# Differences of inputs, some low parts of weights and the last group's sums on VectorE, and other times for the weight and input tasks

## The chip, the cores and the metric

The kernel runs on one core of a Trainium2 chip. The metric is the device time of one execution in microseconds (us), lower is better. The kernel before took 955.99 us in the median of three runs (955.51 to 956.83). One more execution was taken with the profiler; all views below are of that one.

## What is computed

Three parts follow each other: attention with exponential features over 4 batches, 8 heads, 576 positions and 64 dimensions, then two two-layer networks on the 2304 tokens of width 512 that come out of it, with an inner width of 2048. All of it is float32.

```python
def phi(x):
    proj = np.einsum('bhsd,df->bhsf', x, w_phi)
    proj = proj - np.max(np.abs(proj), axis=-1, keepdims=True)
    return np.concatenate([np.exp(proj), np.exp(-proj)], axis=-1)
...
num = np.einsum('bhsf,bhfd->bhsd', phi(q), np.einsum('bhsf,bhsd->bhfd', phi(k), v))
x = num / (den + 1e-6)          # then tokens x 512
h = x @ w_in;   x = (h * sigmoid(h)) @ w_out      # first network
h = x @ w2_in;  y = (h * cos(h)) @ w2_out         # second network
```

## The kernel before, in words

**The three parts.** Attention fills the first 167 us or so and is not touched by the change, but tasks of the first network already run between its pieces. The two networks are the two layers of `moe` (layer 0 and layer 1 in the code; the text calls them layer 1 and layer 2). Nearly all of the span after attention is matmuls of TensorE (PE).

**Precision and products.** A float32 operand is held as two reduced-precision tiles: a high part, which is a copy into the type `fp32r`, and a low part, which is the operand minus the high part. A product then takes three matmuls (high-high, high-low, low-high; `products`, lines 746 to 753). The first matrix product of a layer is done with a Strassen-like scheme of seven block products instead of eight. The scheme needs sums and differences of blocks on both sides: of the weights (`S1`, `S2`, `S3`, `S4`, made by `add` inside `in_tasks`, line 230, in the tile `stage`) and of the tokens (`T1` to `T4`, made by `diff` inside `Inputs.build`, line 560, in tiles `tt`). Each of them is then split into a high part, which the scalar engine (ACT) copies, and a low part: for weights in `Weights.split` (ACT line 186, low part line 189 on GpSimd, POOL), for tokens in `split` inside `Inputs.build` (ACT line 570, low part line 573 on VectorE, DVE, in tiles `xo`).

**The order of the steps.** The inner width is cut in four groups (`NG` = 4). For each layer the token blocks 0, 1 and a small one run through the four groups, then the blocks 2 and 3. One block in one group is a step (`step`, line 910; `small`, line 885, for the small block). A step makes its seven products in PSUM tiles `h`, applies the activation (`act`; in layer 2 the cosine goes over DVE line 776, ACT line 777, and DVE lines 780 to 782), and multiplies by the second weight matrix into tiles `y`, which are added into `xa` (ACT line 854 for the first group, DVE line 856 after that). Inside a step ACT copies the first product into a second bank as soon as it is there (line 936); the third product that PE starts waits for that copy. DVE sums two banks in lines 954 and 965.

**What sets the order on the engines.** The kernel's schedule is written by hand (`manual_schedule`): each engine executes in the order in which the program issues. Beside the steps there are tasks: converting weights from the 64-bit inputs (`convert`: ACT line 166, DVE lines 167, 172 and 178), summing and splitting them (tasks named "in" for the first matrix and "out" for the second, with `put` making the two parts and saving them to DRAM), and building token blocks ("build0", "build1", "buildS"). A clock `weights.now` counts 7 units in a step and 4 in a small step, `at[layer, group, block]` is its value at a step's start. At certain points of a step `fill()` runs all tasks whose time has come, in order of time; a task can also ask that another was done a number of units ago (`after`). If a weight or a token block is needed and not made yet, its tasks are run on the spot. So the times that `plan` (line 998) gives to the tasks decide where in the queues of ACT, DVE, POOL and SyncE (SP) their instructions stand.

```python
def fill():
    weights.flush()
    loads()
    tasks.run(weights.now)
    weights.now += 1
```

The layer-2 weights (`STORED`) are converted while the last group of layer 1 runs, the last quarter of them in layer 2, and are read back from DRAM.

## Time and profile before

| | |
|---|---|
| three runs, median | 955.99 us (955.51 to 956.83) |
| profiled execution | 956.93 us |
| its span on the core | 955.1 us |
| mean granted TensorE clock | 0.996 of full speed |
| chain that ended last, by engine | PE 85%, DVE 7%, ACT 2%, DMA 2%, POOL 1% |

The span is what the profiler sees between the first and the last instruction; the device time is 1.8 us longer. Busy time is the sum of an engine's instruction durations; PEld is the load of weights into TensorE, which overlaps with the matmuls. The chain is followed back from the last instruction, at each step to what released it; a share of a chain is not a saving. A wait in the list of waits is idle time of an engine just before an instruction, put down to the event that came last. Rows of a timeline show in brackets how long the engine was idle before, and who released it.

### The profile page before, as it was taken

The page shows a single profiled execution, that of the slowest core. Times are in us where ns is not written, and L with a number is a line of the kernel's source. Part 1 is how long each engine was busy: PE and PEld are TensorE (multiplying, and loading weights), DVE is VectorE, ACT ScalarE, POOL GpSimd, SP SyncE. Part 2 cuts the span into 40 slices and gives each one's busy share as a digit, 9 for nine tenths or more (in the row PEclk, how much of TensorE's full clock was granted, in tenths as well). Part 3 has the DMA queues.
Part 4 walks back from the last instruction along what each step waited for, and adds up shares of the span by engine and source line. Part 5 has one row for each costly group of instructions (what it writes and reads, how often), then busy time and mean ns, then how long its engine had stood idle before and what let it go on. Part 6 is the DMA issues. An engine that isn't in the chain of part 4 may idle for free.

```text
span 955.1 us, 18114 instructions
## 1 busy us (share of the span) xinstructions
PE 935.0 (98%) x7271; PEld 817.4 (86%) x7271; DVE 635.1 (66%) x913; ACT 520.4 (54%) x944; POOL 237.8 (25%) x190
## 2 busy tenths in 40 slices
PE   8999999899999999999999999999899999999998
PEld 7777776788899898889988898988789898888996
DVE  5777566785737558965465667488876778566556
ACT  4667766665535355565544456564554556644442
POOL 0112352335433423822502621002320120000000
PEclk9999999999999999999999999999999999999999
DMA  5653655566636479797797866352538366242302
GB/s 166 207 142 102 192 171 143 189 224 233 219 151 237 162 228 337 272 324 293 292 323 267 303 252 239 132 178 89 192 133 271 121 232 216 99 171 89 132 1 88
DMA packets 95492, 186.53 MB, mean 195 GB/s; under 512 B 27953, under 2 KB 56753, under 8 KB 94641
## 3 DMA queue, kind: packets, MB, share of 16 engines
q1 hardware_dynamic: 95264, 185.25, 57.0%
q8 instruction: 57, 0.93, 0.4%
q14 instruction: 27, 0.21, 0.1%
q10 hardware_dynamic: 144, 0.13, 0.0%
HBM read 128.06 MB, written 57.22 MB: 194 GB/s over the span
## 4 chain that ended last, share of the span: by engine, by line
PE 85%; DVE 7%; DMA 2%; ACT 2%; issue 2%; POOL 1%; SPq 0%; DVEq 0%; POOLq 0%; ACTq 0%
PE h L752 34%; PE y L828 6%; PE y L827 6%; PE y L826 6%; PE y L821 6%; PE y L823 6%; PE y L822 6%; PE p L377 3%; PE num L455 3%; PE kv L436 3%; PE t L407 2%; PE num L466 2%; DVE xo L573 2%; PE kv L433 1%; PE t L369 1%
## 5 line engine op out<-in xcount | busy, mean ns | idle before, releaser
L752 PEld LDWEIGHTS h<-xo,w 128*128 128x128 f32 x2688 | 332.1, 189 | 20.1 <-ACT h L936 7.1
L752 PE MATMUL h<-xo,w 128*128 128x256 f32 x2688 | 337.7, 282 | 9.7 <-ACT h L936 5.7
L821 PE MATMUL y<-gh,w 128*128 128x512 f32 (+1 forms) x320 | 119.5, 374 | 1.9 <-ACT xa L854 1.4
L823 PE MATMUL y<-gh,w 128*128 128x512 f32 (+1 forms) x320 | 118.8, 371 | 0.0
L822 PE MATMUL y<-gl,w 128*128 128x512 f32 (+1 forms) x320 | 118.7, 371 | 0.0
L828 PE MATMUL y<-w,gl 128*128 128x512 f32 x288 | 113.9, 396 | 0.0
L827 PE MATMUL y<-w,gh 128*128 128x512 f32 x288 | 113.6, 394 | 0.0
L826 PE MATMUL y<-w,gh 128*128 128x512 f32 x288 | 113.4, 394 | 0.0
L189 POOL TENSOR_TENSOR w<-wt,w 128x512 fp32r<-128x512 f32 x32 | 45.9, 1437 | 235.7 <-ACT w L186 220.7
L777 ACT ACTIVATE tb<-tb 128x512 f32<-128x512 f32 x72 | 45.6, 634 | 99.1 <-DVE tb L776 99.1
L772 DVE TENSOR_TENSOR gl<-ta,gh 128x512 fp32r<-128x512 f32 x72 | 63.9, 888 | 53.5 <-ACT gh L770 53.4
L189 POOL TENSOR_TENSOR w<-stage,w 128x512 fp32r<-128x512 f32 x56 | 78.1, 1402 | 74.9 <-ACT w L186 57.2
L776 DVE SCALAR_TENSOR_TENSOR tb<-tb,ta 128x512 f32<-128x512 f32 x72 | 52.2, 725 | 55.8 <-ACT tb L786 55.8
L856 DVE TENSOR_TENSOR xa<-y,xa 128x512 f32<-128x512 f32 (+1 forms) x114 | 70.1, 656 | 26.3 <-PE y L823 19.7
L821 PEld LDWEIGHTS y<-gh,w 128*128 128x128 f32 x320 | 60.2, 188 | 11.8 <-ACT xa L854 1.6
L823 PEld LDWEIGHTS y<-gh,w 128*128 128x128 f32 x320 | 60.1, 188 | 11.4 <-POOL w L189 0.2
L822 PEld LDWEIGHTS y<-gl,w 128*128 128x128 f32 x320 | 60.1, 188 | 9.3
L828 PEld LDWEIGHTS y<-w,gl 128*128 128x128 f32 x288 | 54.0, 188 | 13.2 <-DVE gl L782 0.4
L827 PEld LDWEIGHTS y<-w,gh 128*128 128x128 f32 x288 | 54.0, 188 | 10.7
L826 PEld LDWEIGHTS y<-w,gh 128*128 128x128 f32 x288 | 54.1, 188 | 10.5
L770 ACT CAST gh<-ta 128x512 fp32r<-128x512 f32 x72 | 44.7, 621 | 24.9 <-PE y L823 23.0
L782 DVE TENSOR_TENSOR gl<-tb,gh 128x512 fp32r<-128x512 f32 x72 | 52.8, 733 | 2.8
(102 smaller groups left out, 1411.0 us busy)
## 6 DMA issues: line engine op xcount, KB each, us to landing
w<-d SPq DMA_DIRECT2D x48, 512.0 KB, 5.6
raw_in<-in_moe_w_in SPq DMA_DIRECT2D x32, 512.0 KB, 5.0
raw_out<-in_moe_w_out SPq DMA_DIRECT2D x32, 512.0 KB, 4.9
d<-w SPq DMA_DIRECT2D x32, 512.0 KB, 4.7
rb<-rd SPq DMA_DIRECT2D x16, 288.0 KB, 4.2
va<-in_v SPq DMA_DIRECT2D x32, 128.0 KB, 6.0
yd<-xa SPq DMA_DIRECT2D x4, 1024.0 KB, 4.4
xo<-yd SPq DMA_DIRECT2D x32, 128.0 KB, 6.1
```

The lines of the kernel that those rows point to most:

```text
L189: nc.gpsimd.tensor_sub(lo, t, hi.bitcast(F32))
L752: nc.tensor.matmul(dst[:, ab], w[:, a, ab, c * P:(c + 1) * P], o[:, b, idx, c], start=start and n == 1, stop=n == 12, skip_group_check=True)
L772: return [silu, lambda: nc.vector.tensor_sub(lo, a, hi.bitcast(F32))]
L776: nc.vector.scalar_tensor_tensor(b, b, MAGIC, a, op0=ALU.subtract, op1=ALU.subtract)
L782: nc.vector.tensor_sub(lo, b, hi.bitcast(F32))
L821: nc.tensor.matmul(o, w[:, 0, at], hi[:, f, x], stop=False, **st)
L822: nc.tensor.matmul(o, w[:, 0, at], lo[:, f, x], start=False, stop=False)
L823: nc.tensor.matmul(o, w[:, 1, at], hi[:, f, x], start=False, stop=en)
L826: nc.tensor.matmul(o, hi[:, f, at], w[:, 0], stop=False, **st)
L827: nc.tensor.matmul(o, hi[:, f, at], w[:, 1], start=False, stop=False)
L828: nc.tensor.matmul(o, lo[:, f, at], w[:, 0], start=False, stop=en)
L856: nc.vector.tensor_tensor(v, o, v, op=ALU.add)
```

## The change

The change touches the engine and the time of work beside the products. All four differences of a token block now go to DVE (line 563; before, DVE did two of them for blocks 0 and 1 of layer 1, POOL the rest). The low parts of weights (line 189) go to DVE while the clock is between 0 and the first small step, which are the first two steps, and from one unit after the start of layer 2; elsewhere they stay on POOL. The sums of weights (line 232) go to DVE in the second of these times only. The rest of the change gives other start and end times to the tasks, and the first difference of a token block that is loaded from DRAM asks for 3.5 units after its load instead of 4; since the clock only counts whole units between the calls, this acts as 4.

```diff
@@ class Weights
+        self.lows, self.sums_at = (), ()
...
@@ split
-        nc.gpsimd.tensor_sub(lo, t, hi.bitcast(F32))
+        e = nc.vector if any(a <= self.now < b for a, b in self.lows) else nc.gpsimd
+        e.tensor_sub(lo, t, hi.bitcast(F32))
...
@@ in_tasks, add
-                (nc.gpsimd.tensor_sub if minus else nc.gpsimd.tensor_add)(at(o), at(a), at(b))
+                e = nc.vector if any(a <= self.now < b for a, b in self.sums_at) else nc.gpsimd
+                (e.tensor_sub if minus else e.tensor_add)(at(o), at(a), at(b))
...
@@ Inputs.build
-        def diff(n, a, b, engine):
+        def diff(n, a, b):
             def go():
                 tmp[n] = temps()
-                engine.tensor_sub(part(n), part(a), part(b))
+                nc.vector.tensor_sub(part(n), part(a), part(b))
...
-        d, g = nc.vector if dram is None else nc.gpsimd, nc.gpsimd
-        t1, t2, t4, t3 = diff("T1", "12", "11", d), diff("T2", "22", "T1", d), diff("T4", "21", "T2", g), diff("T3", "22", "12", g)
+        t1, t2, t4, t3 = diff("T1", "12", "11"), diff("T2", "22", "T1"), diff("T4", "21", "T2"), diff("T3", "22", "12")
         if loads:
-            after(loads[-1], 4, t1)
+            after(loads[-1], 3.5, t1)
...
@@ moe
+        weights.lows = (0, at[0, 0, SMALL]), (at[1, 0, 0] + 1, n)
+        weights.sums_at = weights.lows[1:]
...
@@ plan
-                    a, b = at[0, NG - 1, 0] + 2, at[0, NG - 1, 3] + 2
-                    ends = (a + (b - a) * g / 3, a + (b - a) * (g + 1) / 3) if g < 3 else (at[1, 0, SMALL], at[1, 2, SMALL])
+                    a, b = at[0, NG - 1, 0] + 2.5, at[0, NG - 1, 3] + 3
+                    ends = (a + (b - a) * g / 3, a + (b - a) * (g + 1) / 3) if g < 3 else (at[1, 0, SMALL] - 4, at[1, 2, SMALL] - 1)
...
-                tasks.add("in", ins[:12], *((b0 + 1, b1 - 1) if (l, g) != (0, 1) else (b0 + 6, b1 + 3)))
-                tasks.add("in", ins[12:21], b1 - 1, b1 + 6)
-                tasks.add("in", ins[21:], b1 + 6, bs + 3)
-                tasks.add("out", outs[:3], b1, b1 + 6)
-                tasks.add("out", outs[3:], bs + 1, nx + 6.5)
+                tasks.add("in", ins[:12], *((b0 + 2.5, b1 + 5) if (l, g) != (0, 1) else (b0 + 6.5, b1 + 6.5)))
+                tasks.add("in", ins[12:21], b1 - 3, b1 + 6)
+                tasks.add("in", ins[21:], b1 + 8.5, bs + 1)
+                tasks.add("out", outs[:3], b1 - 2, b1 + 7.5)
+                tasks.add("out", outs[3:], bs + 0.5, nx + 6.5)
...
-            tasks.add("build1", b[2:], 3, 8)
+            tasks.add("build1", b[2:], -2.5, 7)
...
-            for tag, src, used, start in (((0, 2), xd[2], at[0, l, 0], at[0, l, 1] + 2),
-                                               ((0, 3), xd[3], at[0, l, 1], at[0, l, SMALL] + 2),
-                                               ((1, 0), yd[0], at[0, l, 2], at[0, l, 3] + 1),
-                                               ((1, 1), yd[1], at[0, l, 3], at[1, 0, 0]),
-                                               ((1, 2), yd[2], at[1, l, 0], at[1, l, 1] + 2),
-                                               ((1, 3), yd[3], at[1, l, 1], at[1, l, SMALL] + 2)):
+            for tag, src, used, start, end in (((0, 2), xd[2], at[0, l, 0], at[0, l, 1] + 2, 5.5),
+                                               ((0, 3), xd[3], at[0, l, 1], at[0, l, SMALL] + 2, 9.5),
+                                               ((1, 0), yd[0], at[0, l, 2], at[0, l, 3] + 3, 1),
+                                               ((1, 1), yd[1], at[0, l, 3], at[1, 0, 0] + 1, 8),
+                                               ((1, 2), yd[2], at[1, l, 0], at[1, l, 1] + 0.5, 4.5),
+                                               ((1, 3), yd[3], at[1, l, 1], at[1, l, SMALL] - 2, 10)):
...
-                tasks.add(name, b[4:], start, start + 7)
-            for n, t in enumerate((at[0, 0, 1] + 2, at[0, 0, 3])):
+                tasks.add(name, b[4:], start, start + end)
+            for n, t in enumerate((at[0, 0, 1] + 2.5, at[0, 0, 3] + 1.5)):
...
-        for name, n, end in (("in", 1, 0), ("out", 2, 6)):
+        for name, n, end in (("in", 1, 0), ("out", 2, 6.5)):
...
-            tasks.add(name, todo[n:], 3, end)
+            tasks.add(name, todo[n:], 2.5, end)
```

In the listings below a row is a line of the program, an operation, out<-in and the shape; lines of the changed kernel are 1 to 5 higher for the same statement (563 is 566, 573 is 576, 167 is 168, 172 is 173, 178 is 179, 189 is 191, 232 is 235, 305 and 308 are 308 and 311, 772 is 777, 776 is 781, 780 to 782 are 785 to 787, 854 is 859, 936 is 941, 965 is 970).

**First excerpt: DVE in the second step** (layer 1, group 0, block 1). `xo_2452` is this block's tile of high and low parts, `xn` and `rb` belong to the last head of attention, `wt` and `stage` to weights. Before:

```order
L573 TENSOR_TENSOR xo_2452<-xa,xo_2452 128x512
L178 SCALAR_TENSOR_TENSOR wt<-ws,wt 128x512
L772 TENSOR_TENSOR gl<-ta,gh 128x2x256
L573 TENSOR_TENSOR xo_2452<-tt,xo_2452 128x512
L167 TENSOR_SCALAR wt<-raw_out 128x512
L172 SCALAR_TENSOR_TENSOR wt<-raw_out,wt 128x512
L305 TENSOR_TENSOR xb<-xn,rb 128x4x128 x2
L308 TENSOR_TENSOR xa<-xn,rb 128x2x64
L573 TENSOR_TENSOR xo_2452<-xa,xo_2452 128x512
```

Of the change:

```order
L576 TENSOR_TENSOR xo_2452<-xa,xo_2452 128x512
L576 TENSOR_TENSOR xo_2452<-tt,xo_2452 128x512
L566 TENSOR_TENSOR tt<-xa 128x512
L191 TENSOR_TENSOR w_2449<-wt,w_2449 128x512
L168 TENSOR_SCALAR wt<-raw_out 128x512
L173 SCALAR_TENSOR_TENSOR wt<-raw_out,wt 128x512
L308 TENSOR_TENSOR xb<-xn,rb 128x4x128 x2
L311 TENSOR_TENSOR xa<-xn,rb 128x2x64
L576 TENSOR_TENSOR xo_2452<-xa,xo_2452 128x512
L179 SCALAR_TENSOR_TENSOR wt<-ws,wt 128x512
L576 TENSOR_TENSOR xo_2452<-tt,xo_2452 128x512
L168 TENSOR_SCALAR stage<-raw_in 128x2x256
```

The block's third low part (its second from `xa`) is the last row before and the first row of the change: it has moved ahead of the three operations of attention's last head. A difference and a low part of a weight (`w_2449`) are new on this queue, and the row after these is a further low part, `w_2450`.

**Second excerpt: ACT after the small block's step of the first group.** The rows of lines 854 and 859 bring the output products to `xa`; the `w_` rows are copies of weights. Before:

```order
L854 COPY xa<-y 128x4x128 x2
L186 CAST w_2651<-wt 128x512
L186 CAST w_2652<-stage 128x512
L186 CAST w_163<-stage 128x512
L186 CAST w_164<-stage 128x512
L186 CAST w_165<-stage 128x512
L166 ACTIVATE ws<-raw_out 128x512
L769 ACTIVATE ta<-h 128x512
L770 CAST gh<-ta 128x2x256
L854 COPY xa<-y 128x4x128 x2
```

Of the change:

```order
L859 COPY xa<-y 128x4x128 x2
L187 CAST w_2655<-stage 128x512
L187 CAST w_2656<-stage 128x512
L187 CAST w_2657<-wt 128x512
L167 ACTIVATE ws<-raw_out 128x512
L774 ACTIVATE ta<-h 128x512
L775 CAST gh<-ta 128x2x256
L859 COPY xa<-y 128x4x128 x2
L187 CAST w_2658<-stage 128x512
L187 CAST w_163<-stage 128x512
L187 CAST w_164<-stage 128x512
L187 CAST w_165<-stage 128x512
```

Three copies instead of five stand between the two evacuations, and four follow the second one.

**Third excerpt: DVE in layer 2**, in the part of the first group that holds the longest wait. `tb`, `gh` and `gl` are tiles of the cosine, `stage` holds the weights to be summed. Before:

```order
L776 SCALAR_TENSOR_TENSOR tb<-tb,ta 128x512
L780 TENSOR_TENSOR tb<-tb,u 128x512
L781 CAST gh<-tb 128x2x256
L782 TENSOR_TENSOR gl<-tb,gh 128x2x256
L167 TENSOR_SCALAR wt<-raw_out 128x512
L776 SCALAR_TENSOR_TENSOR tb<-tb,ta 128x512
```

Of the change:

```order
L781 SCALAR_TENSOR_TENSOR tb<-tb,ta 128x512
L168 TENSOR_SCALAR wt<-raw_out 128x512
L785 TENSOR_TENSOR tb<-tb,u 128x512
L786 CAST gh<-tb 128x2x256
L787 TENSOR_TENSOR gl<-tb,gh 128x2x256
L235 TENSOR_TENSOR stage<-stage 128x512
L781 SCALAR_TENSOR_TENSOR tb<-tb,ta 128x512
```

A sum of weights has come to the place ahead of the second cosine step, and the shift of line 167 stands earlier.

## Rows read from the trace of the kernel before

**Rows 1.** The page's part 1: engine, busy us (share of the span), instructions.

```profile
PE 935.0 (98%) x7271; PEld 817.4 (86%) x7271; DVE 635.1 (66%) x913; ACT 520.4 (54%) x944; POOL 237.8 (25%) x190
```

**Rows 2.** Busy time by stretches; columns in the first line.

```profile
core 0: us, PE busy (x) PEld busy (x) DVE busy (x) ACT busy (x) POOL busy (x), PEclk, DMA share, GB/s
165.00:200.00 35.00, 30.52 (x228) 26.19 (x217) 27.92 (x42) 24.19 (x45) 13.24 (x11) 1.00 0.64 202
200.00:230.00 30.00, 28.61 (x184) 25.88 (x183) 19.28 (x24) 18.25 (x33) 17.91 (x12) 1.00 0.61 224
230.00:370.00 140.00, 140.00 (x940) 128.59 (x939) 86.89 (x132) 71.90 (x127) 47.88 (x36) 1.00 0.60 211
370.00:415.00 45.00, 43.48 (x302) 39.98 (x301) 41.17 (x48) 26.81 (x49) 31.41 (x21) 1.00 0.88 303
415.00:560.00 145.00, 145.00 (x903) 130.09 (x902) 81.64 (x116) 71.71 (x126) 48.45 (x34) 1.00 0.83 298
560.00:585.00 25.00, 23.95 (x157) 21.61 (x157) 19.74 (x31) 15.96 (x27) 6.06 (x4) 1.00 0.73 274
672.00:700.00 28.00, 24.90 (x151) 22.53 (x151) 20.96 (x28) 15.52 (x26) 8.40 (x6) 0.94 0.41 154
700.00:800.00 100.00, 100.00 (x622) 89.20 (x621) 76.92 (x115) 50.86 (x82) 16.30 (x12) 1.00 0.59 195
```

**Rows 3.** PE's waits: line waited for: us in total, times, longest us.

```profile
PE h L752 <- ACT h L936: 5.7, 4, 3.1
PE h L752 <- DVE xo L573: 2.1, 2, 1.7
PE y L821 <- ACT xa L854: 1.4, 1, 1.4
```

**Rows 4.** Timeline of PE in the first step: start, duration, instruction, [idle before].

```profile
171.82 5.94 PE L752 MATMUL h<-xo,w 128*128 128x256 f32 x48 [0.68 <-ACT h L936]
178.55 0.62 PE L752 MATMUL h<-xo,w 128*128 128x256 f32 x3 [0.78 <-DVE u L965]
```

**Rows 5.** Busy time (columns as in rows 2) after two of PE's waits.

```profile
580.84:585.38 4.54, 4.54 (x37) 4.54 (x38) 3.15 (x6) 3.56 (x6) 0.00 (x0) 1.00 0.82 307
691.29:697.35 6.06, 6.06 (x37) 6.06 (x38) 2.60 (x5) 3.50 (x6) 1.28 (x1) 0.72 0.28 116
```

**Rows 6.** Instructions on tile tt: ns min/median/max, first and last start.

```profile
L573 DVE TENSOR_TENSOR xo<-tt,xo x32: 676/684/1787, 163.9 to 799.4; 128x512 fp32r<-128x512 f32 x32
L563 POOL TENSOR_TENSOR tt<-xo x12: 1292/1302/1677, 356.6 to 792.0; 128x512 f32<-128x512 f32 x12
L563 DVE TENSOR_TENSOR tt<-xa x2: 685/686/686, 156.0 to 172.2; 128x512 f32<-128x512 f32 x2
```

**Rows 7.** Timeline ahead of the longest wait, all engines (columns as in rows 4).

```profile
681.77 1.78 DVE L776 SCALAR_TENSOR_TENSOR tb<-tb,ta 128x512 f32<-128x512 f32 x1
...
684.80 1.29 POOL L189 TENSOR_TENSOR w<-stage,w 128x512 fp32r<-128x512 f32 x1 [1.80 <-ACT w L186]
...
684.98 1.41 DVE L781 CAST gh<-tb 128x512 fp32r<-128x512 f32 x1
...
686.06 3.14 POOL L232 TENSOR_TENSOR stage<-stage 128x512 f32<-128x512 f32 x2
...
686.42 1.67 DVE L782 TENSOR_TENSOR gl<-tb,gh 128x512 fp32r<-128x512 f32 x1
...
688.00 1.48 DVE L167 TENSOR_SCALAR wt<-raw_out 128x512 int32<-128x512 int32 x1
...
690.66 0.58 ACT L936 COPY h<-h 128x512 f32<-128x512 f32 x1
```

**Rows 8.** ACT's waits (columns as in rows 3).

```profile
ACT h L936 <- PE h L752: 65.2, 25, 5.0
...
ACT w L186 <- POOL stage L232: 11.3, 8, 2.4
...
ACT xo L570 <- POOL tt L563: 7.8, 5, 4.2
```

**Rows 9.** Timeline of ACT, the weight copies behind the small block's products.

```profile
219.33 0.62 ACT L186 CAST w<-stage 128x512 fp32r<-128x512 f32 x1 [2.00 <-POOL stage L232]
```

## The prediction

> **What bounds the kernel now.** The page's busy times come first: TensorE (PE) is busy 935.0 of 955.1 us [rows 1], so nothing that leaves its matmuls alone can save more than 20 us, and the question is where its idle 20 us lie. The table by stretches answers it for the two layers. PE is idle 35.00 - 30.52 = 4.48 us from 165 to 200, 1.39 us from 200 to 230, 1.52 us from 370 to 415, 1.05 us from 560 to 585 and 3.10 us from 672 to 700 [rows 2]; in the stretches between them that the same table shows, PE has no idle time up to 800. The list of PE's waits names who ended them: the ScalarE (ACT) copy of line 936 four times for 5.7 us, the VectorE (DVE) low part of line 573 twice for 2.1 us and an ACT evacuation (line 854) once for 1.4 us [rows 3]. No weight load is in that list.
>
> Two of these waits belong to the first step, where PE has nothing else to do between a product and its copy: 0.68 us at 171.82 for the copy of line 936 and 0.78 us at 178.55 for the DVE sum of line 965 [rows 4]. Their order does not change, so they stay. That leaves 4.48 - 0.68 - 0.78 = 3.02 us in the first stretch.
>
> The longest wait costs more than itself. From 691.29, when it ends, 37 matmuls take 6.06 us at a mean granted clock of 0.72; the same 37 after the 1.05 us wait at 580.84 take 4.54 us at full clock [rows 5]. So 6.06 - 4.54 = 1.52 us are the price of running at 1.2 GHz instead of 2.4 for a while after 3.10 us of idleness, and they go with the wait.
>
> **Why these engines are late.** One DVE operation of 128x512, the low part from a difference, takes 0.684 us in the median and 1.787 us at worst; a difference takes 0.685 us on DVE and at least 1.292 us on GpSimd (POOL) [rows 6]. The slow DVE cases are those beside POOL work. From 684.98 to 689.4 a cast, a subtraction and a shift take 1.41, 1.67 and 1.48 us, while POOL does a low part (684.80) and two sums of the last weight group (686.06, 3.14 us); only then does the DVE step of line 776 start, and the ACT copy that PE waits for starts at 690.66 [rows 7]. Two-input operations on POOL thus cost twice: their own time and about 1 us of each DVE operation that they meet. ACT also waits on POOL directly: 7.8 us for differences (longest 4.2) and 11.3 us for sums [rows 8].
>
> **The change, part by part.** It moves 48 operations from POOL to DVE: 28 differences (all of them), 16 low parts of weights (5 in the first two steps, 11 in layer 2) and the 4 sums of the last group. No matmul, copy or DMA is added or removed; PE's order is the same, while weight work, saves and weight loads shift by a few places in the queues of ACT, DVE, POOL and SyncE (SP).
>
> *First two steps, 165 to 200.* Without POOL work here the stretched operations fall back to 0.68, and the low part that PE awaited at 190.41 now stands ahead of three operations of the attention's last head (first excerpt). The third moved low part (w_2450) stands on DVE behind an ACT copy that is itself behind three ACT operations of some 0.62 us (as the weight copy in [rows 9]), so DVE is held up to 1.9 us, with the sum of line 965 behind it. This costs PE between 0 and 1.9 us; I take 0.5, the lower part, as PE has output products to do before it needs that sum. Gain 3.02 - 0.5 = 2.5 us.
>
> *Small block, 200 to 230.* The evacuation is late because ACT's queue holds five weight copies before it, and one of them waits 2.00 us for POOL's sum of line 232 [rows 9]. In the new order three stand there, and four more come after it (second excerpt). Gain 1.39 us. The weights they make are then some 3 us later, but PE needs them only in the middle of the next step. Bounds: nothing, or 1.39 us.
>
> *Differences of stored blocks.* In 370 to 415 six differences leave POOL's 21 operations and come to DVE, which is busy 41.17 of 45 us [rows 2]. They add 6 x 0.69 = 4.1 us and take off about as many stretches of 1 us, so DVE's load hardly moves; what goes is the round trip DVE, POOL, ACT, DVE. I take half of the 1.52 us: 0.76, between 0 and 1.52. In 560 to 585 POOL's differences are all of its work, DVE has 5 us free, and the 1.05 us wait (an ACT copy behind a cast that waited for a POOL difference) goes whole. A difference on DVE could also hold that queue for its block's load: each stands two evacuations into the following step, by which time POOL had long had the data, so this costs nothing here; if a load were late, everything of DVE behind it would be.
>
> Against this part speaks a rule. The row is DVE's 91% from 370 to 415. The Trainium skill, "Perfetto Trace Analysis", section "Optimizing Scalar/DVE Operations", says that work may be offloaded to GpSimd if DVE is saturated, and that it might not help between these two because they share a read port. By its first half this part would cost 4.1 us instead of giving 0.76; by its second half it would give about 0. The trace bears out the second half in the stretched operations.
>
> *Layer 2, 560 to 800.* Low parts and sums of the last group go to DVE, so POOL has nothing left after about 560. A sum costs DVE 0.69 where it met about 1 us of stretching per sum before. The chain from 681.77 has eight steps (line 776, ACT's sine, lines 780, 781 and 782, one sum, line 776, sine; third excerpt). At an unstretched 0.69 us each [rows 6] it ends at 687.3, the copy of 0.58 us [rows 7] at 687.9, and PE wants it at 691.29 - 3.10 = 688.2. The wait of 3.10 and the 1.52 of half clock go: 4.62 us. The bound below is nothing, if another wait takes its place. The 11 low parts add 11 x 0.69 = 7.6 us to a DVE that has far more idle time there, 23 us between 700 and 800 alone [rows 2]; I cost them at nothing, and their waits on ACT are the slower rival.
>
> *Task times* move sums later (1.5 units after the small block begins) and builds closer together; I cost these at nothing beyond the above.
>
> Sum: 2.5 + 1.39 + 0.76 + 1.05 + 4.62 = 10.3 us. The profiled execution took 956.93 us, so 946.6. It lies 0.94 above the median of the runs shown; I keep this as an allowance for one new wait of the common size (0.85 to 1.05 us) and forecast **946.6 us**.
>
> **Rivals.**
> *The long wait stays* (chance 0.14). The copy of line 936 still stands behind an ACT sine that waits for DVE's line 776, and a sum now stands just before that (third excerpt). For it: DVE is in order and each low part waits for ACT. Against it: the unstretched chain has 0.3 us to spare, and more if its cast is shorter than 0.69. Then 10.3 - 4.62 = 5.7 us remain: 951.2 us.
>
> *DVE becomes the bound from 370 to 415* (0.11). The 4.1 us come on top, with no stretch given back, because POOL keeps its 15 weight operations there. Gain 10.3 - 0.76 - 4.1 = 5.4: 951.5 us. The first half of the sentence from the Trainium skill's "Perfetto Trace Analysis" would have it so.
>
> *Nothing lasting* (0.05). POOL keeps 72 of 88 low parts, and the moved times make as many waits as they end: about 956.
>
> *Slower: low parts hold DVE* (0.07). A low part on DVE waits for its ACT copy, which can stand behind the copy of line 936, and ACT waits there for PE 65.2 us in 25 waits, 2.6 us each [rows 8]. In layer 2 the DVE operations behind are those that ACT's sine and PE's next products need. If all 11 passed on the full 2.6 us, that would be 28.7 us; from 0.94 us each it outweighs the gain. With half of it, 14.3 us, the time is 956.9 - 10.3 + 14.3 = 961. Against it: in the order read, such a low part is followed by a step of line 776 that waits for a later ACT operation anyway.
>
> **The numbers.** The forecast has 0.63. A measurement of this kernel can tell about 0.2% (1.9 us) from no change. Faster by more than that, below 954.1: 0.63 + 0.14 + 0.11 = 0.88; within: 0.05; slower: 0.07. The low end takes all that can go, 11.6 us, off the median, and most of the allowance: 943.5. The high end holds the two weaker gains: 952.0. Outside lie the last two cases and a little of the others.
>
> **What would show it.** Right: PE without waits over 0.3 us at the places of 190, 224, 580 and 691; the granted clock at full from 672 to 700; POOL with no work after some 560; the low parts of line 573 (now 576) at most 0.7 us in the first steps and layer 2. The 0.68 and 0.78 us of the first step still there. Wrong: a new PE wait on line 965's sum or on the copy of line 936 in layer 2, DVE waiting for ACT's weight copies by more than 1 us at a time with PE idle after it, or stretched DVE operations where POOL is idle, which would take the whole mechanism away.

## The result, and the profile after

The changed kernel took **941.75 us** in the median of four runs (940.53 to 944.05), the kernel before 955.75 us beside it: a ratio of 0.9856, 95% interval 0.9834 to 0.9878. The gain is 14.0 us by the medians; the forecast of 946.6 us lies only 9.2 below the same 955.75, and the measured time lies below the range of 943.5 to 952.0. In a later comparison, on another occasion, the same kernel took 943.20 us against 956.47, ratio 0.9872 (0.9850 to 0.9894).

The profiled execution took 941.50 us, with a span of 939.4 us. First the busy times, the line that answers to [rows 1]:

```profile
PE 929.7 (99%) x7271; PEld 813.9 (87%) x7271; DVE 639.5 (68%) x961; ACT 522.3 (56%) x944; POOL 173.2 (18%) x142
```

48 operations went from POOL to DVE, POOL lost 64.6 us of work, and DVE gained 4.4, not 48 x 0.69 = 33: the operations it has anyway became shorter. The changed kernel runs ahead, by 2 us at 165 and by 15 at 700, so the same times hold other work. The next rows are therefore taken over the same matmuls as five of the stretches of [rows 2] (165 to 200, 200 to 230, 370 to 415, 560 to 585 and 672 to 700), with the same columns:

```profile
162.73:194.16 31.43, 29.99 (x228) 26.14 (x217) 27.30 (x46) 23.12 (x42) 2.44 (x5) 1.00 0.59 195
194.16:222.65 28.49, 28.49 (x184) 25.89 (x183) 20.10 (x26) 20.16 (x36) 15.34 (x11) 1.00 0.61 205
...
362.17:404.69 42.52, 42.52 (x302) 39.79 (x301) 37.03 (x51) 26.12 (x48) 20.87 (x14) 1.00 0.87 303
...
549.77:573.74 23.97, 23.97 (x157) 21.65 (x157) 20.04 (x33) 14.83 (x25) 0.00 (x0) 1.00 0.85 323
661.18:684.80 23.62, 23.31 (x151) 20.83 (x151) 19.34 (x33) 15.44 (x26) 0.00 (x0) 1.00 0.54 189
```

PE is idle 1.44 us in the first of them, which is the first step's pair of waits (0.66 and 0.78 us), and 0.31 us in the last. POOL has no work in layer 2. What is left of PE's waits (columns of [rows 3]):

```profile
PE kv L436 <- DMA vt<-in_v: 1.6, 1, 1.6
...
PE h L757 <- DVE u L970: 1.1, 2, 0.8
PE h L757 <- ACT h L941: 0.7, 1, 0.7
...
PE h L757 <- DVE xo L576: 0.3, 1, 0.3
```

Both programs issue the same 7271 matmuls in the same order, so the two traces can be laid on each other matmul by matmul. The lead of the changed kernel is how much earlier it starts the same matmul, counted from the start of each span. It grows in these places; the last column is the prediction's term.

| place (times of before) | lead gained, us | forecast, us |
|---|---|---|
| attention, 150 to 157 | 2.2 | 0 |
| first steps, 165 to 200 | 3.6 | 2.5 |
| small block, 200 to 230 | 1.5 | 1.39 |
| 230 to 370 | 0.5 | 0 |
| 370 to 415 | 2.5 | 0.76 |
| 415 to 560 | -0.1 | 0 |
| 560 to 672 | 0.6 | 1.05 |
| 672 to 700 | 4.4 | 4.62 |
| 700 to the end | 0.5 | 0 |
| sum | 15.7 (as the spans: 955.1 - 939.4) | 10.3 |

### The profile page after: what moved, and what is told of

It is laid out like the page before. It is cut to its first block, busy times and chain, and to the rows that moved or that the text cites. A ratio compares the mean times of both kernels' runs of the same rounds, so it can differ in the third digit from the quotient of the medians.

```text
span 939.4 us, 18064 instructions
## 1 busy us (share of the span) xinstructions
PE 929.7 (99%) x7271; PEld 813.9 (87%) x7271; DVE 639.5 (68%) x961; ACT 522.3 (56%) x944; POOL 173.2 (18%) x142
## 4 chain that ended last, share of the span: by engine, by line
PE 97%; DMA 1%; DVE 1%; ACT 1%; issue 0%; SPq 0%
PE h L757 38%; PE y L826 7%; PE y L828 7%; PE y L827 7%; PE y L833 7%; PE y L832 7%; PE y L831 7%; PE p L380 4%; PE num L458 3%; PE kv L439 3%; PE t L410 2%; PE num L469 2%; PE kv L436 1%; PE t L372 1%; DMA vt<-in_v 0%; DMA wf<-in_w_phi 0%
## 5 line engine op out<-in xcount | busy, mean ns | idle before, releaser
L757 PEld LDWEIGHTS h<-xo,w 128*128 128x128 f32 x2688 | 330.0, 188 | 11.6 <-DVE u L970 2.2
L781 DVE SCALAR_TENSOR_TENSOR tb<-tb,ta 128x512 f32<-128x512 f32 x72 | 49.3, 685 | 48.9 <-ACT tb L791 48.9
L191 POOL TENSOR_TENSOR w<-stage,w 128x512 fp32r<-128x512 f32 x48 | 66.7, 1400 | 42.3 <-ACT w L187 36.3
L191 POOL TENSOR_TENSOR w<-wt,w 128x512 fp32r<-128x512 f32 x24 | 39.7, 1656 | 125.6 <-ACT w L187 125.6
L235 POOL TENSOR_TENSOR stage<-stage 128x512 f32<-128x512 f32 x28 | 40.7, 1454 | 82.2 <-DVE stage L179 81.8
```

Source lines behind the costliest of these rows:

```text
L191: e.tensor_sub(lo, t, hi.bitcast(F32))
L757: nc.tensor.matmul(dst[:, ab], w[:, a, ab, c * P:(c + 1) * P], o[:, b, idx, c], start=start and n == 1, stop=n == 12, skip_group_check=True)
L781: nc.vector.scalar_tensor_tensor(b, b, MAGIC, a, op0=ALU.subtract, op1=ALU.subtract)
```

## The experiments

Three theories were set against each other. **A**: the engine counts; two-input work on POOL stretches DVE's operations and makes ACT wait. **B**: the new task times ended the waits. **C** came after the first four runs: the two need each other, and where an operation stands decides. Each kernel was timed beside the kernel before, on the same chip. The 95% interval of a ratio reaches some 0.2%, or 2 us, to either side, so the times alone do not settle smaller differences between two kernels. A gain over the kernel before is worked out from the ratio unless it is said to be one of medians; the two are up to 1.3 us apart. Line numbers are those of each kernel.

### The changed kernel again

No edit.

> The changed kernel once more, on the same chip as the three others, as their base. Theory (waits of TensorE that ended) and every rival: 941.75 us as measured before, in the bounds 940.5 to 944. A question of its own: the wait on the DMA of vt near 152 us took 2.28 us and was followed by some 1.3 us of half clock before the change, and took 1.56 us with no half clock after it. If the change has nothing to do with it, this run may show either of the two; if the change shortened it, it is 1.56 us again.

Measured: 943.20 us (941.80 to 946.51), ratio 0.9872 (0.9850 to 0.9894). PE's wait on the loads of `vt` was 2.8 us this time:

```profile
PE kv L436 <- DMA vt<-in_v: 2.8, 1, 2.8
```

So one and the same program shows 1.6 and 2.8 us; in the profiles of all kernels that leave this part as it was, the wait takes between 0.8 and 2.8 us. Its length is chance, and so are the 2.2 us of lead that the first pair of profiles shows there. Without them the change is worth 15.7 - 2.2 = 13.5 us in these profiles; the medians of the two timed comparisons give 14.0 and 13.3, their ratios 13.8 and 12.2.

### The moves alone, and the times alone

```diff
 # e2: before, with the hunks of Weights, split, add, diff and lows/sums_at;
 #     plan() and its times as before
 # e3: before, with the hunks of plan() and of the first in and out tasks;
 #     split, add and diff as before
```

> The kernel before with the 48 operations on VectorE, and the old task times. Theory A (the engine is what counts: two-input work on GpSimd stretches VectorE's operations and makes ACT wait): the waits near 190, 410, 580 and 691 end, the one of 1.39 us near 224 stays, since its sums stay on GpSimd; 13.4 us without the part before 165 us less the 1.6 us there, so some 11.5 us faster than before, 944 us. Rival B (the new task times are what ended the waits): within 2 us of before, 954 to 956 us.

> The kernel before with the new task times, and all operations on the engines they had. Theory A: only the wait near 224 ends (1.39 us of idle, 1.55 us from one product to the next), and the long wait near 691 stays in some form: 953 to 955 us. Rival B: 942 to 946 us, with the wait near 691 gone.

Measured: the moves alone 958.20 us, ratio 1.0025 (1.0009 to 1.0041), so **slower** by some 2.4 us. The times alone 951.14 us, ratio 0.9944 (0.9928 to 0.9961), 5.4 us faster. Both together give 12 to 14. Neither theory stands: added up, the two alone give 3 us, so some 9 us come only from the two together. PE's waits with the moves alone:

```profile
PE h L757 <- ACT h L941: 4.9, 4, 2.2
PE h L757 <- DVE xo L576: 4.0, 2, 3.2
PE y L831 <- DVE gh L786: 1.7, 2, 1.0
```

The waits between 370 and 415 are gone, but 3.2 us are new in the second step, 1.05 us near 580 have become 2.2 (at 578.9), there are new waits of 0.5 to 0.7 us near 630, and near 690 two of 1.0 and 1.5 us stand in place of the long one. The timelines of DVE and then of ACT in the second step show how the longest comes about:

```profile
188.85 0.69 DVE L173 SCALAR_TENSOR_TENSOR stage<-raw_in,stage 128x512 int32<-128x512 int32 x1
191.32 0.69 DVE L191 TENSOR_TENSOR w<-wt,w 128x512 fp32r<-128x512 f32 x1 [1.77 <-ACT w L187]
191.93 0.68 DVE L179 SCALAR_TENSOR_TENSOR stage<-ws,stage 128x512 int32<-128x512 int32 x1
192.53 0.68 DVE L576 TENSOR_TENSOR xo<-xa,xo 128x512 fp32r<-128x512 f32 x1
```

```profile
189.04 0.58 ACT L947 COPY u<-h 128x512 f32<-128x512 f32 x1
189.52 0.60 ACT L774 ACTIVATE ta<-h 128x512 f32<-128x512 f32 x1
190.15 0.62 ACT L775 CAST gh<-ta 128x512 fp32r<-128x512 f32 x1
190.67 0.61 ACT L187 CAST w<-wt 128x512 fp32r<-128x512 f32 x1
```

The moved low part (line 191) needs ACT's copy, which stands behind three operations of the step. DVE waits 1.77 us for it, and behind it in DVE's queue waits the low part that PE needs next (line 576, at 192.53; PE goes on at 193.27 after 3.2 us of idle, so DVE's wait is more than half of PE's). This is the mechanism of the prediction's slower rival. In layer 2 such waits of DVE for ACT's copy stand before 682.94 (1.98 us) and 687.83 (1.21 us).

With the times alone the waits are other ones:

```profile
PE h L752 <- ACT h L936: 5.0, 3, 2.6
...
PE y L821 <- DVE xa L856: 1.1, 1, 1.1
PE y L823 <- POOL w L189: 1.0, 1, 1.0
```

The wait of 1.39 us of the small block is gone, and so, unforeseen, is the long one of 3.10 us near 691, though POOL still does the sums. New ones of 1.05 to 2.57 us stand at 190, 197, 385 and 558. Waits near these places are there again, below, when the differences or the first low parts alone are POOL's.

### The differences back on POOL

```diff
-        def diff(n, a, b):
+        def diff(n, a, b, engine):
...
-                nc.vector.tensor_sub(part(n), part(a), part(b))
+                engine.tensor_sub(part(n), part(a), part(b))
...
+        d, g = nc.vector if dram is None else nc.gpsimd, nc.gpsimd
 # ... and the four calls of diff with the engines that they had
```

> The changed kernel with the differences of token blocks where they were (26 of 28 on GpSimd). Theory A: the 2.5 us of 370 to 415 and the 0.6 us of 560 to 590 come back, some part of the 3.6 us of the second step (one or two differences of its block) too: 945 to 947 us, and stretched VectorE operations beside the differences. Rival B: 942 us as the changed kernel, since the times are kept.

Measured: 948.24 us, ratio 0.9927 (0.9909 to 0.9944); the changed kernel in the same comparison took 943.20, so with the new times the differences' move is worth 5 us. The waits are at 186.85 (1.40 us), 379.72 (1.04) and 553.19 (2.55):

```profile
PE h L758 <- ACT h L942: 5.3, 3, 2.5
...
PE y L827 <- DVE xa L862: 1.0, 1, 1.0
```

The size was as theory A has it or a little above, the places only partly: the new times had moved the blocks' differences, and with POOL as their engine they wait at 553 instead of 580.

### Layer 2's low parts and sums back on POOL; the first steps' low parts back on POOL

```diff
 # e5
-        weights.lows = (0, at[0, 0, SMALL]), (at[1, 0, 0] + 1, n)
-        weights.sums_at = weights.lows[1:]
+        weights.lows = ((0, at[0, 0, SMALL]),)
+        weights.sums_at = ()
 # e6
+        weights.lows = ((at[1, 0, 0] + 1, n),)
+        weights.sums_at = weights.lows
```

> The changed kernel with the 11 low parts and 4 sums of layer 2 on GpSimd again, times and differences as changed. The prediction's step: with these sums beside VectorE the long wait near 691 returns, up to 3.10 us of idle and 1.5 us of half clock, 946 to 948 us. Theory C (after the run with the times alone, which has GpSimd's sums and no wait there): the long wait was ended by the new place of the sums, not by their engine, so nothing over 0.5 us of idle in layer 2: 943 us, within 1 us of the changed kernel.

> The changed kernel with the 5 low parts of the first two steps on GpSimd again, all else as changed. Theory C: the wait of 1.05 us of TensorE on GpSimd's low part near 196, which the run with the times alone shows, returns, with 0.2 to 0.3 us around it that is no idle time: 944 to 945 us. Rival: it was the differences that GpSimd did just before that made it late, and they are on VectorE now, so no wait: 943 us as the changed kernel.

Measured, layer 2 back on POOL: 940.78 us, ratio 0.9854 (0.9837 to 0.9871), the same as the changed kernel. No wait of layer 2 comes back, though POOL's sums are slow and stretch DVE beside them (a cast of 0.43 us takes 1.40 at 670.09). POOL's last sums (columns as in rows 7), then the stretch 672 to 700:

```profile
667.65 3.55 POOL L235 TENSOR_TENSOR stage<-stage 128x512 f32<-128x512 f32 x2
```

```profile
672.00:700.00 28.00, 28.00 (x174) 24.91 (x173) 23.09 (x34) 16.40 (x27) 6.79 (x5) 1.00 0.52 191
```

They end at 671.2, 6.4 us before PE wants the copy (the matmul that waited before starts at 677.57 here). In the kernel before they ran from 686.06 to 689.20 [rows 7], over the moment at which PE wanted it. So 15 of the 48 moves, to which the prediction gave its largest term, brought nothing measurable. Matmul by matmul they even cost 0.7 us: two small new waits of the changed kernel, at 668 and 775, are missing here.

With the first low parts back on POOL: 943.48 us, ratio 0.9876 (0.9860 to 0.9893). The trace has the waits back, 1.10 us at 189.43 and 0.49 us at 195.59 on POOL's low part itself:

```profile
PE h L757 <- ACT h L941: 1.8, 2, 1.1
...
PE y L828 <- POOL w L191: 0.5, 1, 0.5
```

Matmul by matmul this kernel gains 1.7 us from 165 to 200, where the changed kernel gains 3.6; so these low parts are worth some 2 us in the trace. The measured times (943.48 beside 941.75 and 943.20) can't tell it from nothing.

### POOL work that nobody waits for

The changed kernel, with 54 POOL operations on a tile of their own that nothing else reads, one behind the other from some 540 us on: additions of the tile to itself in the first run (until 614 us), a multiplication by 1 and addition of 0 in the second (until 594).

```diff
+        idle = [sp.tile([P, 2 * TH], F32, name=f"idle{i}") for i in range(1)]
...
         def fill():
...
+            if at[1, 0, 0] <= weights.now < at[1, 3, 0]:
+                nc.gpsimd.tensor_add(idle[0], idle[0], idle[0])
 # e8, in its place:
+                nc.gpsimd.tensor_scalar(idle[0], idle[0], 1.0, 0.0, op0=ALU.mult, op1=ALU.add)
```

> The changed kernel, with 54 additions of a 128x512 tile to itself on GpSimd that nobody waits for, which run one behind the other from about 541 us on, some 70 us. Theory A on the stretch (two-input work on GpSimd slows VectorE's operations, whoever waits for it): VectorE's operations of 0.69 us take 1.4 to 1.8 us there and no longer than 0.69 after it; VectorE has 19 to 21 us of work in 25 there, so it becomes the bound and the time grows by 10 to 30 us, to 953 to 973. Rival (the long VectorE operations come from something else, as DMA traffic, and GpSimd only costs those that wait for it): 943 us, and VectorE's durations as they were.

> The same with 54 one-input operations (the tile times 1 plus 0) in place of the additions. If it is GpSimd's being busy that slows VectorE, VectorE's operations stretch as in the run with two inputs, 953 to 973 us. If it takes two inputs on GpSimd, they keep 0.69 us and the time is 943 us. I have no run that speaks for either, and hold the second for somewhat likelier.

Measured: two inputs 971.53 us, ratio 1.0168 (1.0150 to 1.0186), about 29 us more than the changed kernel; one input 952.13 us, ratio 0.9970 (0.9957 to 0.9983), about 10 us more; that one input costs nothing had been held likelier, and it does cost. DVE's groups (mean ns behind the comma) in the changed kernel and with two inputs from 541 to 611, then with one input from 544 to 593, while that work lasts:

```profile
L576 DVE TENSOR_TENSOR xo<-tt,xo 128x512 fp32r<-128x512 f32 x8 | 5.5, 685 | 0.3 <-ACT xo L573 0.3
...
L786 DVE CAST gh<-tb 128x512 fp32r<-128x512 f32 x10 | 4.3, 427 | 0.5
...
L861 DVE TENSOR_TENSOR xa<-y,xa 128x512 f32<-128x512 f32 x4 | 2.6, 682 | 0.0
```

```profile
L576 DVE TENSOR_TENSOR xo<-tt,xo 128x512 fp32r<-128x512 f32 x8 | 12.1, 1523 | 0.0
...
L791 DVE CAST gh<-tb 128x512 fp32r<-128x512 f32 x6 | 6.0, 1005 | 0.2
...
L866 DVE TENSOR_TENSOR xa<-y,xa 128x512 f32<-128x512 f32 x4 | 2.5, 675 | 0.0
```

```profile
L576 DVE TENSOR_TENSOR xo<-tt,xo 128x512 fp32r<-128x512 f32 x7 | 7.6, 1092 | 0.0
...
L791 DVE CAST gh<-tb 128x512 fp32r<-128x512 f32 x5 | 3.8, 766 | 0.2
...
L866 DVE TENSOR_TENSOR xa<-y,xa 128x512 f32<-128x512 f32 x4 | 2.5, 675 | 0.0
```

Nothing waits for this POOL work, and DVE still takes 1.52 us for a low part of 0.685. So the stretch is real and belongs to POOL's activity. It spares one kind of operation: `xa<-y,xa`, which reads one operand from PSUM, keeps its 0.675 us in both runs. The Trainium skill, "SBUF — State Buffer", section "SBUF: two separate sides", says that DVE and GpSimd share one pair of ports under an exclusive lock, and that a DVE operation needs it if it has two SBUF inputs (or runs in a two-port mode). The trace agrees: with two inputs on POOL, 1523 ns for the low part, which has two SBUF inputs, against 675 for `xa<-y,xa`. The busy times of the stretch, in the changed kernel, with two inputs, and with one:

```profile
541.00:611.00 70.00, 69.75 (x435) 62.23 (x434) 50.83 (x84) 41.16 (x70) 0.43 (x1) 1.00 0.65 231
```

```profile
541.00:611.00 70.00, 50.32 (x258) 43.98 (x257) 66.78 (x57) 25.78 (x44) 65.92 (x53) 0.84 0.41 150
```

```profile
544.00:593.00 49.00, 42.28 (x244) 37.51 (x243) 44.83 (x52) 23.38 (x39) 44.62 (x54) 0.93 0.61 223
```

DVE is full with two inputs (66.78 of 70 us) and does 57 operations where the changed kernel does 84 in the same 70 us.

### One line of times alone, and the differences alone

The line of the first run starts the weight tasks of the last group of layer-2 weights 4 units earlier and ends them 1 unit earlier; their sums and low parts stay on POOL.

```diff
 # e9: before, and
-                    ends = (a + (b - a) * g / 3, a + (b - a) * (g + 1) / 3) if g < 3 else (at[1, 0, SMALL], at[1, 2, SMALL])
+                    ends = (a + (b - a) * g / 3, a + (b - a) * (g + 1) / 3) if g < 3 else (at[1, 0, SMALL] - 4, at[1, 2, SMALL] - 1)
 # e10: before, and
-                engine.tensor_sub(part(n), part(a), part(b))
+                nc.vector.tensor_sub(part(n), part(a), part(b))
```

> The kernel before with one line of the change alone: the weight tasks of the last stored group start 4 units and end 1 unit earlier; nothing is moved to another engine. Theory C (the long wait near 691 was ended by the sums' place in the order, not by their engine): no wait of over 0.5 us between 672 and 700, and the other waits as before: 4.6 us less than before, about 951 us. The prediction's step (it takes the move to VectorE): the wait stays or only shifts, 955 to 956 us.

> The kernel before with the 28 differences on VectorE and nothing else, with the old task times. If the new waits of the run with all moves and old times belong to the low parts of weights (VectorE stands 1.2 to 2.0 us at a time for ACT's copy), they are not here: the waits of 0.85 us and 0.50 us between 370 and 415 end, the one near 580 grows from 1.05 to 2.2 us as it did there, and the long one stays: 954 to 955 us. If the differences themselves don't fit the old times, it is slower than before: 957 to 960 us.

Measured, one line of times: 952.31 us (948.29 to 954.39), ratio 0.9948 (0.9928 to 0.9968), 5.0 us less than before (3.8 by the medians) where 4.6 were expected. In its trace the long wait is the only one of layers 1 and 2 that is missing, and matmul by matmul it gains 4.8 us at that place and 0.2 after it; what else it gains or loses (2.9 us at the loads of `vt`, -0.7 in the first step) lies before any instruction that the line moves. POOL does the same two sums, but earlier:

```profile
676.01 3.54 POOL L232 TENSOR_TENSOR stage<-stage 128x512 f32<-128x512 f32 x2
```

```profile
672.00:700.00 28.00, 28.00 (x175) 24.86 (x174) 24.70 (x37) 15.62 (x26) 8.99 (x7) 1.00 0.51 186
```

PE is busy 28.00 of 28 us at full clock where it had 24.90 at 0.94 [rows 2]. Theory C holds: the place of this group's work ended that wait, with the sums still on POOL. The line also moves the group's conversions, copies and low parts; that it was the sums among them is argued from [rows 7] and not shown by itself.

The differences alone: 953.99 us (950.63 to 957.33), ratio 0.9979 (0.9964 to 0.9994), 2.0 us less, as expected. The long wait stays (3.09 us), the one near 580 is 2.20 us as with the moves alone:

```profile
PE h L751 <- ACT h L935: 6.0, 3, 3.1
PE h L751 <- DVE xo L573: 2.3, 2, 1.3
```

With the old times the differences are worth 2 us, with the new ones 5. The 2.2 us near 580 thus come from the differences at the old times; the waits of DVE for ACT's weight copies, which this run does not have, come from the low parts. With the low parts and the sums, that is with all the moves, the kernel is 4.4 us slower than this one.

This run shows one thing more. The same 36 matmuls behind the same long wait, in the kernel before and here:

```profile
691.29 6.06 PE L752 MATMUL h<-xo,w 128*128 128x256 f32 x36 [3.10 <-ACT h L936]
```

```profile
686.68 4.51 PE L751 MATMUL h<-xo,w 128*128 128x256 f32 x36 [3.09 <-ACT h L935]
```

They run at full clock here after the same idle time. So the 1.52 us of half clock that the prediction books with this wait do not follow it in every execution. The eleven other executions of this kernel had a mean clock of 0.995 to 0.998, so the profiled one, with 1.000, is not the usual case.

### A version from what was learnt, and more of the same

```diff
 # e11: as e5, and in attention
+        def load_t(n):
+            b, h0 = divmod(n, 2)
+            h0 *= 4
             for i in range(4):
                 a, z = divmod(i, 2)
                 nc.sync.dma_start(vt[n % 2][64 * z:64 * z + 64, a, z * W:z * W + D], v[b, h0 + i, SM:S, :])
...
-load.q++ qx.2+ x.7++ ...
+load.q++ load.t++ qx.2+ x.7++ ...
 # e12: the changed kernel, and
-        weights.lows = (0, at[0, 0, SMALL]), (at[1, 0, 0] + 1, n)
-        weights.sums_at = weights.lows[1:]
+        weights.lows = weights.sums_at = ((0, n),)
```

> A version put together from the runs so far: the changed kernel with layer 2's low parts and sums left on GpSimd, as in the run of 940.78 us, and the small loads of vt (the tail rows of v) of a head issued one head earlier, where the wait of TensorE on them near 152 us took 0.8 to 2.8 us in the profiles so far. Expected: that wait gone, 938 to 940 us, if nothing else is late there; if the loads of va that follow are late next, 940 to 941 us.

> The changed kernel with all low parts and sums of weights of both layers on VectorE, so GpSimd does nothing after the first step. No VectorE operation is stretched any more, but 72 low parts more can make VectorE wait for ACT's copies, 1.2 to 2.0 us at a time as seen in the run with the old times, and from 370 to 415 it gets some 10 us more of work. If these waits fall where TensorE needs VectorE, 945 to 955 us; if the stretched operations were what they cost, 941 to 942 us. I hold the first for likelier.

Measured: the first took **938.98 us** (938.77 to 940.49), ratio 0.9820 (0.9801 to 0.9839), faster than before and than the changed kernel: its interval lies below that of the changed kernel in the comparison of 943.20 us (from 0.9850) and touches the one of 941.75 (from 0.9834), and its slowest execution (940.49) is no slower than the fastest of that kernel's eight (940.53). What the loads of `vt` gave of it over the 940.78 us of the run without them is 1.8 us, less than the times can settle. The wait on `vt` is gone, and the one on `va` behind it takes 0.5 us:

```profile
PE kv L443 <- DMA va<-in_v: 0.5, 1, 0.5
```

The second took 945.26 us (941.25 to 946.11), ratio 0.9873 (0.9852 to 0.9895): the low end of what was expected, and by its interval the same as the changed kernel. The times don't settle whether more of the same costs anything; the traces say that it costs some 2.4 us. DVE's waits for ACT's weight copies, in the changed kernel, then in this one:

```profile
DVE w L191 <- ACT w L187: 11.8, 7, 3.0
```

```profile
DVE w L191 <- ACT w L187: 64.3, 30, 5.9
```

Matmul by matmul, this kernel gains 1.5 us between 230 and 585, where the changed kernel gains 3.9, and one new wait of PE over 0.2 us stands there (0.85 us at 548.4). So 52.5 us more of waiting on DVE, and the operations added to it, cost PE only 2.4. DVE's waiting for ACT is not a cost in itself; it becomes one where PE needs what stands behind it.

## Why the prediction was right or wrong

**Two steps failed.** The mechanism failed where the task times were put at nothing; this does not show in the sum. The number failed where a wait of TensorE was priced at its idle time; this put the time below the range, for the low end of the range already counted every wait in full, at that price.

**Right: where the time was.** Each of PE's waits that the prediction listed between 185 and 700 is gone, the pair of 0.66 and 0.78 us of the first step is still there, the clock is full from 672 to 700, and the stretched operations are what theory A says (1.52 us against 0.685 with nobody waiting). That pair is less fixed than the prediction took it: the first of the two was 0.68 us in the kernel before and 1.27 to 1.36 in the three other profiles that have the differences on POOL, and 0.66 in all ten that have them on DVE. Over the 302 matmuls that ran from 370 to 415 before, DVE's load fell from 41.17 to 37.03 us, with all of the token blocks' differences there now on DVE, so the rival that DVE becomes the bound there had the wrong sign. This is the second half of the rule of the Trainium skill's "Perfetto Trace Analysis", section "Optimizing Scalar/DVE Operations": that moving work between the two might not help because they share a read port. The prediction's count there is off by one: POOL's 21 operations held seven differences, one begun before 370, and 14 weight operations, not six and 15.

**Wrong: the task times, "I cost these at nothing beyond the above".** The moves with the old times are 2.4 us slower, and one line of the times is worth 5.0 us by itself. The terms were read from order excerpts of the changed kernel, which hold the new times, so the sum has their effect in it without saying so. The times decide whether a low part on DVE comes after ACT has made its copy, and whether the last group's weight work runs over the moment at which PE wants a copy.

**Wrong: the cause of the largest term.** The term of 4.62 us for 672 to 700 had the right size (4.4, with 0.6 of a new small wait taken off; 5.0 timed), but it was put down to the engine of the sums and low parts. With that line of times alone, sums on POOL, it is gained; with all of layer 2's work back on POOL, nothing is lost; and with the moves alone, at the old times, the same matmuls gain 1.3 us and those just before them lose 1.9. So that the term came out was luck: the change also held the line that earns it. The order excerpts showed the sum's new place; what was not asked is how far the old place lay from the moment of need. The 1.52 us of half clock in the term also do not go with the wait each time, as the differences alone showed.

**Wrong: the price of a wait.** The sum took a wait at its idle time. The stretch of the three waits in the second step shows more; the same matmuls, before and after:

```profile
188.29:195.27 6.98, 3.97 (x30) 3.36 (x28) 6.84 (x12) 2.71 (x7) 1.45 (x2) 1.00 0.69 239
```

```profile
186.01:189.44 3.43, 3.43 (x29) 3.24 (x28) 3.40 (x8) 3.07 (x7) 0.00 (x0) 1.00 0.22 91
```

Idle time is 6.98 - 3.97 = 3.01 us, the difference 6.98 - 3.43 = 3.55 us: 0.18 us more per wait. For the waits at 386, 410, 580 and 691 it is some 0.26 us each (at 580: 1.32 us between the same matmuls for 1.05 of idle). Two places between 230 and 370 have no idle time in the list at all and still gave 0.2 us each. The low end of the range took 11.6 us as "all that can go"; the same waits gave back 13.8, matmul by matmul (3.6 + 1.5 + 2.5 + 1.3 + 4.9). Why a wait costs more than its idle time is not shown.

**Mis-sized: two cautious terms.** The 0.5 us kept back in the second step were not needed: the low part of `w_2450` stands at 190.23 on DVE with no wait before it. And half of the 1.52 us from 370 to 415 was taken; all of it went, with its surplus 2.5 us. The 0.94 us kept as an allowance for a new wait were about right, in other form: new small waits at 572, 581, 668 and 775 took 1.6 us.

**The slower rival** had 0.07. Its mechanism is real and is what the moves alone show (958.2 us, where the rival had 961); whether it strikes is decided by the times of the tasks.

**Open.** Which other lines of the times matter was not tried one by one, nor where the first low parts' 2 us lie in the times.

## What to carry to other kernels

On engines that run in order, an operation's engine and its place are one choice: before a move, read on the new queue what it will wait for and who stands behind it, and ask of every long operation how far it lies from the moment at which the bounding engine needs its neighbours. Two-input work on GpSimd is paid twice where VectorE has two-input work on SBUF, so look for a place in time where VectorE is not needed before looking for another engine. Here a wait of TensorE cost its idle time and 0.2 to 0.3 us more; let the same matmuls in two traces tell what a wait cost.

## What was not expected of the hardware

A one-input operation on GpSimd stretches VectorE too, by less: 1.09 us for a low part of 0.685, where two inputs make it 1.52. An operation with an operand in PSUM is not touched (0.675 us).

After idle times of TensorE of nearly the same length the granted clock differs. Behind the long wait near 691 the kernel before and the run with the differences alone show it (6.06 and 4.51 us for the same 36 matmuls, after 3.10 and 3.09 us of idle). Right behind the wait on `vt` the mean was 0.58 of full speed over 4.05 us in the kernel before (after 2.28 us of idle), 0.50, that is 1.2 GHz, with the times alone (after 2.70) and 1.00, or 2.4 GHz, in the changed kernel's second profile (after 2.78); the columns are those of rows 2:

```profile
152.94:156.99 4.05, 4.04 (x64) 3.60 (x65) 3.57 (x6) 2.20 (x7) 0.00 (x0) 0.58 0.36 129
```

```profile
153.28:156.00 2.72, 2.72 (x38) 2.53 (x38) 1.93 (x4) 0.43 (x1) 0.00 (x0) 0.50 0.67 198
```

```profile
153.59:156.20 2.61, 2.61 (x66) 2.38 (x68) 1.83 (x4) 1.19 (x6) 0.00 (x0) 1.00 0.72 206
```

So a single profile can hold some 1.5 us of lost clock that another profile does not have after the same wait, and a wait of 2 to 3 us is to be priced with both.
